# Where the two parts of a head pair's value product stand in the attention loop, and the order of four small copies

## The chip, the cores and the metric

The kernel runs on one core of a Trainium2 chip. The metric is the device time of one execution in microseconds (us). A core has TensorE (PE in the profile; PEld is its weight load), VectorE (DVE), ScalarE (ACT), GpSimd (POOL) and SyncE (SP), each with its own instruction stream, which it works through in order. TensorE writes its results to PSUM, which has eight banks.

## The reference

```
scores = q @ k.T / sqrt(64) + decay            # decay from cumsum(log f); causal mask
attn   = softmax(scores)                       # 4 batches x 8 heads, 576 x 576
x      = attn @ v                              # laid out as 2304 tokens x 512
h = x @ w_in;   x = (h * clip(h + 3, 0, 6) / 6) @ w_out
h = x @ w_in2;  out = (max(h, 0) + alpha * min(h, 0)) @ w_out2
```

All inputs are float32; both feed-forward layers have 2048 inner columns. The change touches the attention alone, in the line `x = attn @ v`.

## The kernel before

The 32 heads are worked in 16 pairs, and each pair is cut into nine **units** of query rows: four units of 128 rows for the first head, one **tail unit** that holds the last 64 rows of both heads, and four units for the second head. They are called u0 to u3, u4 (the tail) and u5 to u8 here. A unit goes through a pipeline that is spread over the steps of one loop (`for t in range(...)`). In step t each engine is given, in the order of the letters in `ORD = "TMEVDS"`:

- T, the transposes of unit t-5 on TensorE (`transposes`, line 419; the tail unit also has a small fifth one, `tq`, line 423);
- M, the negated row maximum of unit t-1 on VectorE (`maxes`, line 364);
- E, the exponential of unit t-2 on ScalarE (`exps`, line 371), which also sums each row;
- V, the copies of the transposed unit t-5 out of PSUM (`evac`): on VectorE for u3 and u8, on ScalarE for all others (`EV`);
- D, what a finished pair still needs, at fixed distances from its last unit: `recips` (RD = 3), `spread` (SD = 6; transposes `tr` and `tj` on TensorE, then three ScalarE copies, lines 456 and 460), and the value product `stage3` in two parts (PA = 7 and PB = 9);
- S, the scores of unit t on TensorE (`stage1`, lines 388 to 390, for the tail 400 to 404).

So while one pair's scores and softmax run, the pair before it is finished. In the text, "u1" to "u8" are the units of the running pair, and the value product that stands among them belongs to the pair before.

The value product's first part covers query rows 0 to 255 (four matmuls in the program), the second rows 256 to 575 (ten). Each matmul gives one head's 64 output channels, so a weight tile has 64 columns and the two heads' matmuls fill the two halves of the array (`128*64` in the profile). Everything else in the loop uses tiles of 128 columns. Most of these float32 matmuls show twice in the profile. After each part VectorE multiplies the result with the reciprocal row sums into `r` (line 480).

The eight PSUM banks are dealt out so:

- four hold scores. `score_banks` hands them out in turn, one per unit and two for the tail, ten per pair, and a score matmul waits for the exponential that last read its bank (`reader`). By that count u7 and u8 get the two banks that u4 had, u6 the bank of u3, and u5 the bank of u2;
- three form the ring `ps_pt` (tag `tp`): each unit's transposes take the next one, so do `tq`, `tr` and `tj`; a new tile waits until the tile three places earlier has been read;
- one, `ps_pv`, holds the value product.

Weight conversion and the building of the feed-forward's operands are set between these steps by tables of step numbers; in all pairs but the last ScalarE's share of them is given out behind u6's exponential. The feed-forward runs after the attention.

Of the kernel before, what the change touches and what calls it, by code (L numbers as in the profile page):

```python
# [8 lines left out]
F32 = mybir.dt.float32  # L9
# [12 lines left out]
def decay_attention_ffn2_kernel(ctx, tc, qk, v, f, wi1, wo1, wi2, wo2, alpha, out):  # L22
    nc = tc.nc
    NHEAD = qk.shape[0]
    S = f.shape[1]
# [3 lines left out]
    NP = B * NPAIR  # L29
# [11 lines left out]
    TAIL = S - 512  # L41
    PR = S - 128
    LM, LE, LT, LV = 1, 2, 5, 5
    RD, SD, PA, PB = 3, 6, 7, 9
# [16 lines left out]
    EV = (0, 0, 0, 1, 0, 0)  # L61
# [205 lines left out]
    def x_places(c, t0, t1):  # L267

        got = []
        while t0 < t1:  # L270
            p = t0 // (2 * NB)
            e, o = min(t1, (p + 1) * 2 * NB), 2 * NB * p
            view = R[p].rearrange("p (c t) -> p c t", c=KD)[:, c, t0 - o:e - o]
            got.append((view, t0, e))
            t0 = e
        return got


    def attention():
        with ExitStack() as ax:  # L280
# [28 lines left out]
            ps_pt = ax.enter_context(tc.tile_pool(name="ps_pt", bufs=3, space=PSUM))  # L309
            ps_pv = ax.enter_context(tc.tile_pool(name="ps_pv", bufs=1, space=PSUM))  # L310
# [8 lines left out]
            def load_v(p):  # L319
                vs[p] = vp.tile([128, KT, 128], F32, tag="v", name="vt")  # L320
                nc.sync.dma_start(out=vs[p], in_=v[p // NPAIR, p % NPAIR])
# [21 lines left out]
            def copy_k(h):  # L343
                q1, q2, k1, k2 = slots[h]
                if h >= 4:
                    nc.sync.dma_start(out=k2[0:64].bitcast(F32), in_=k1[0:64].bitcast(F32))
# [60 lines left out]
            def pt_tile(h):  # L407
                if h not in pts:
                    pts[h] = ptp.tile([128, (KT - 1) * PR + S], F32, tag="pt", name="pt")
                return pts[h]  # L410

            def rows(t, n, c0, cw):
                return t[:, c0:c0 + n * PR].rearrange("p (j s) -> p j s", s=PR)[:, :, 0:cw]
# [12 lines left out]
            def evac(u, tp, tq):  # L426
                p, ab, i = u
                if ab < 2:
                    copy = nc.vector.tensor_copy if EV[i] else nc.scalar.copy
                    copy(out=rows(pt_tile(2 * p + ab), i + 1, 128 * i, 128), in_=tp[:, 0:i + 1, :])  # L430
                    return
                for a in range(2):
                    copy = nc.vector.tensor_copy if EV[4 + a] else nc.scalar.copy
                    dst = pt_tile(2 * p + a)
                    copy(out=rows(dst, 4, 512, TAIL), in_=tp[:, :, 64 * a:64 * a + 64])  # L435
                    copy(out=dst[0:TAIL, 4 * PR + 512:4 * PR + S], in_=tq[0:TAIL, 0, 64 * a:64 * a + 64])

            def recips(p):

                ss = sm.pop(p)  # L440
                rc = st.tile([128, 9], F32, tag="rc", name="rc")
                nc.vector.tensor_scalar(out=rc, in0=ss, scalar1=1e-9, scalar2=None, op0=ALU.add)
                nc.vector.reciprocal(out=rc, in_=rc)
                rw = rcp.tile([128, 4, 2, 64], F32, tag="rw", name="rw")
                scaled("P", rw, rc[:, 0:8].rearrange("p (a i) -> p i a", a=2).unsqueeze(3)
                       .broadcast_to([128, 4, 2, 64]))
                rcs[p] = rw, rc

            def spread(p):

                rw, rc = rcs.pop(p)
                t = rcp.tile([128, S], F32, tag="rcb", name="rcb")
                tr = ps_pt.tile([128, 4, 128], F32, tag="tp", name="tr")
                for i in range(4):
                    nc.tensor.transpose(tr[:, i, :], rw[:, i].rearrange("p a b -> p (a b)"), ident)  # L455
                nc.scalar.copy(out=t[:, 0:512], in_=tr.rearrange("p a b -> p (a b)"))
                tj = ps_pt.tile([128, 4, 128], F32, tag="tp", name="tj")
                nc.tensor.transpose(tj[:, 0, :], rc[:, 8:9].broadcast_to([128, 128]), ident)
                for a in range(2):
                    nc.scalar.copy(out=t[64 * a:64 * a + 64, 512:S], in_=tj[64 * a:64 * a + 64, 0, 64 * a:64 * a + 64])  # L460
                rcb[p] = t

            def stage3(p, part):
                b, hp = divmod(p, NPAIR)
                vt = vs[p]
                q0, q1 = ((0, 256), (256, S))[part]
                pv = ps_pv.tile([128, 512], F32, tag="pv", name="pv")
                js = [j for j in range(KT) if 128 * j < q1]
                for j in js:
                    lo = max(q0, 128 * j)  # L470
                    kk = min(128, S - 128 * j)
                    for a in range(2):
                        nc.tensor.matmul(  # L473
                            out=pv[64 * a:64 * a + 64, lo - q0:q1 - q0],
                            lhsT=vt[0:kk, j, 64 * a:64 * a + 64],
                            rhs=pts[2 * p + a][0:kk, j * PR + lo:j * PR + q1],
                            start=(j == js[0]), stop=(j == js[-1]))
                for view, t0, t1 in x_places(hp, b * S + q0, b * S + q1):
                    c0, c1 = t0 - b * S, t1 - b * S
                    nc.vector.tensor_mul(out=view, in0=pv[:, c0 - q0:c1 - q0], in1=rcb[p][:, c0:c1])  # L480
                if part == 1:
                    for d, key in ((vs, p), (rcb, p), (pts, 2 * p), (pts, 2 * p + 1)):
                        d.pop(key)
# [48 lines left out]
            for a in range(2):  # L532
                nc.sync.dma_start(out=aq_d[a, :, 0:2, 576 - 64 * a:640 - 64 * a],
                                  in_=zero[32 * a:32 * a + 32, 0:128].rearrange("p (r c) -> p r c", r=2))
# [59 lines left out]
            for t in range(len(units) + max(LV, PB) + 1):  # L594
                now = todo.pop(t, [])
                for ch in ORD:
                    if ch == "D":
                        for fn in now:
                            fn()
                    if ch == "S" and t < len(units):  # L600
                        live[t] = stage1(units[t])
                    for c, lag, fn in (("M", LM, maxes), ("E", LE, exps)):
                        if ch == c and 0 <= t - lag < len(units):
                            live[t - lag] = fn(*live[t - lag])
                    for c, lag, fn in (("T", LT, transposes), ("V", LV, evac)):
                        if ch == c and 0 <= t - lag < len(units):
                            live[t - lag] = fn(units[t - lag], *live[t - lag])
                if t < len(units):
                    p, ab, i = units[t]
                    pos = t % 9  # L610
                    if ab == 1 and i == 3:
                        for d, fn in ((RD, lambda p=p: recips(p)), (SD, lambda p=p: spread(p)),
                                      (PA, lambda p=p: stage3(p, 0)), (PB, lambda p=p: stage3(p, 1))):
                            todo.setdefault(t + d, []).append(fn)
                    if pos == (2 if p else 8):
                        load_v(p)
                    if pos == QA and 2 * p + 2 < 2 * NP:
                        prep_head(2 * p + 2)
                        todo.setdefault(t + QL, []).append(lambda h=2 * p + 2: low_k(h))
                        todo.setdefault(t + QL, []).append(lambda h=2 * p + 2: copy_k(h))  # L620
                        todo.setdefault(t + QL + 1, []).insert(0, lambda h=2 * p + 2: low_q(h))
                        if p:
                            load_head(2 * p + 3)
                    if pos == QB and 2 * p + 3 < 2 * NP:
                        prep_head(2 * p + 3)
                        for fn, d in ((low_k, QL), (copy_k, QL), (low_q, QL if p else QL + 2)):
                            todo.setdefault(t + d, []).append(lambda fn=fn, h=2 * p + 3: fn(h))
                        if 2 * p + 4 < 2 * NP:
                            load_head(2 * p + 4)
                elif t == len(units) + LE:  # L630
                    rx.close()
                    ffn_open()
                for fn in side.pop(t, []):
                    fn()
                if t < 9:
                    idle(2)
                for _ in range(DRAIN.get(t, 0)):
                    step()
# [244 lines left out]
    def step():  # L883
        return next(runner, None)
# [57 lines left out]
```

## Time and profile before

| | |
|---|---|
| median of 3 runs | 965.91 us (965.73 to 966.28) |
| the profiled execution | 965.22 us, its span 963.4 us |
| busy, PE | 953.9 us, 99% of the span |
| busy, DVE, ACT, POOL | 698.6, 536.3 and 595.3 us |
| granted TensorE clock | 1.00 of full speed in every slice |

"Busy" of TensorE runs from the start of a matmul to a modelled end. Neighbouring matmuls overlap, so an engine that is shown as busy can still be waiting; the distance between the starts of two instructions tells more than the busy time.

### The profile page before, as it was taken

The page shows a single profiled execution, that of the slowest core. Times are in us where ns is not written, and L with a number is a line of the kernel's source. Part 1 is how long each engine was busy: PE and PEld are TensorE (multiplying, and loading weights), DVE is VectorE, ACT ScalarE, POOL GpSimd, SP SyncE. Part 2 cuts the span into 40 slices and gives each one's busy share as a digit, 9 for nine tenths or more (in the row PEclk, how much of TensorE's full clock was granted, in tenths as well). Part 3 has the DMA queues.
Part 4 walks back from the last instruction along what each step waited for, and adds up shares of the span by engine and source line. Part 5 has one row for each costly group of instructions (what it writes and reads, how often), then busy time and mean ns, then how long its engine had stood idle before and what let it go on. Part 6 is the DMA issues. An engine that isn't in the chain of part 4 may idle for free.

```text
span 963.4 us, 15758 instructions
## 1 busy us (share of the span) xinstructions
PE 953.9 (99%) x5525; PEld 858.4 (89%) x5525; DVE 698.6 (73%) x1211; ACT 536.3 (56%) x1316; POOL 595.3 (62%) x583
## 2 busy tenths in 40 slices
PE   8999999999999999999999999999999999999998
PEld 5777777789999999999999999989899898989897
DVE  7888999858687877786788565367788778535454
ACT  5788887765655555464645365545444545443231
POOL 8677989766665566585766299546555669423131
PEclk9999999999999999999999999999999999999999
DMA  6766777300443344211587723414434410344541
GB/s 206 230 188 187 217 241 228 110 30 13 173 186 133 141 186 168 84 44 34 194 318 272 277 77 120 164 46 173 186 101 173 166 64 30 111 188 159 202 164 66
DMA packets 36195, 145.79 MB, mean 151 GB/s; under 512 B 4860, under 2 KB 4860, under 8 KB 33012
## 3 DMA queue, kind: packets, MB, share of 16 engines
q1 hardware_dynamic: 36112, 144.79, 42.6%
q8 instruction: 43, 0.70, 0.3%
q14 instruction: 36, 0.29, 0.1%
q10 hardware_dynamic: 4, 0.00, 0.0%
HBM read 97.21 MB, written 43.42 MB: 146 GB/s over the span
## 4 chain that ended last, share of the span: by engine, by line
PE 93%; POOL 2%; DVE 2%; DMA 1%; issue 1%; ACT 1%; SPq 0%; POOLq 0%; DVEq 0%; ACTq 0%
PE o L772 21%; PE hA L732 20%; PE o L770 19%; PE hC L732 10%; PE hB L732 5%; PE pv L473 5%; PE tp L419 5%; PE sc L388 3%; PE sc L389 2%; PE sc L390 1%; PE sc L400 1%; PE sc L402 1%; PE tr L455 1%; POOL xl L249 1%; DVE r L241 0%
## 5 line engine op out<-in xcount | busy, mean ns | idle before, releaser
L715 POOL TENSOR_TENSOR g<-t,g 128x384 fp32r<-128x384 f32 x192 | 205.9, 1073 | 283.7 <-ACT g L714 267.3
L770 PE MATMUL o<-g,wo 128*128 128x384 f32 x1152 | 230.7, 338 | 1.2 <-POOL g L715 1.1
L732 PE MATMUL hA<-xh,wi 128*128 128x384 f32 x768 | 224.3, 337 | 0.3 <-DVE hD L746 0.3
L772 PE MATMUL o<-wo,g 128*128 128x512 f32 x864 | 223.2, 394 | 0.0
L770 PEld LDWEIGHTS o<-g,wo 128*128 128x128 f32 x1152 | 204.1, 188 | 2.2 <-POOL g L715 1.8
L714 ACT CAST g<-t 128x384 fp32r<-128x384 f32 x192 | 98.9, 515 | 176.7 <-DVE t L709 92.2
L772 PEld LDWEIGHTS o<-wo,g 128*128 128x128 f32 x864 | 160.6, 188 | 25.7
L790 DVE TENSOR_TENSOR r<-o,r 128x512 f32<-128x512 f32 x126 | 86.7, 688 | 86.2 <-PE o L772 85.7
L732 PEld LDWEIGHTS hA<-xh,wi 128*128 128x128 f32 x768 | 141.5, 188 | 3.9 <-DVE hD L746 0.6
L732 PE MATMUL hA<-xl,wi 128*128 128x384 f32 x384 | 129.5, 337 | 0.0
L779 DVE SCALAR_TENSOR_TENSOR r<-o,r 128x384 f32<-128x384 f32 x168 | 92.3, 553 | 47.0 <-PE o L770 46.2
L732 PE MATMUL hC<-xh,wi 128*128 128x384 f32 x384 | 114.1, 338 | 0.0
L371 ACT ACTIVATE p<-sc,nm 128x128 f32<-128x128 f32 (+2 forms) x144 | 80.3, 560 | 16.0 <-DVE nm L364 12.1
L364 DVE TENSOR_REDUCE nm<-sc 128x1 f32<-128x128 f32 (+2 forms) x144 | 71.1, 507 | 11.7 <-PE sc L390 7.5
L732 PEld LDWEIGHTS hA<-xl,wi 128*128 128x128 f32 x384 | 72.1, 188 | 3.2
L732 PEld LDWEIGHTS hC<-xh,wi 128*128 128x128 f32 x384 | 70.9, 188 | 2.1 <-issue 0.2
L249 POOL TENSOR_TENSOR xl<-r,xh 128x384 fp32r<-128x384 f32 x59 | 69.1, 1183 | 2.2 <-ACT xh L244 1.6
L419 PE MATMUL tp<-ident,p 128*128 128x128 f32 x384 | 67.4, 278 | 0.6 <-ACT pt L435 0.6
L737 ACT COPY s<-hA 128x384 f32<-128x384 f32 x96 | 45.9, 478 | 36.2 <-PE hA L732 35.9
L732 PE MATMUL hC<-xl,wi 128*128 128x384 f32 x192 | 64.7, 337 | 0.0
L732 PE MATMUL hB<-xh,wi 128*128 128x384 f32 x192 | 57.1, 338 | 0.0
L746 DVE TENSOR_TENSOR hC<-hC,s 128x384 f32<-128x384 f32 x48 | 27.1, 564 | 40.7 <-PE hC L732 38.8
(143 smaller groups left out, 1744.8 us busy)
## 6 DMA issues: line engine op xcount, KB each, us to landing
wid<-wi SPq DMA_DIRECT2D x24, 896.0 KB
wi<-wid SPq DMA_DIRECT2D x12, 1792.0 KB
rqk<-in_qk SPq DMA_DIRECT2D x32, 608.0 KB
raw<-in_wi SPq DMA_DIRECT2D x32, 512.0 KB
raw<-in_wo SPq DMA_DIRECT2D x32, 512.0 KB
wod<-wo SPq DMA_DIRECT2D x24, 512.0 KB
wo<-wod SPq DMA_DIRECT2D x12, 1024.0 KB
vt<-in_v SPq DMA_DIRECT2D x16, 320.0 KB
```

The lines of the kernel that those rows point to most:

```text
L249: e.tensor_sub(out=XS[k][1][:, b, c], in0=x, in1=XS[k][0][:, b, c].bitcast(F32))
L364: last = waits("V", nc.vector.tensor_reduce(out=nm, in_=src, axis=AX.X if n == 1 else AX.XY, op=ALU.max, negate=True), last)
L371: last = waits("A", nc.scalar.activation(out=o, in_=src, func=AF.Exp, bias=nm, scale=1.0, accum_out=dst), last)
L419: nc.tensor.transpose(tp[:, j, :], pt[:, 128 * j:128 * j + 128], ident)
L473: nc.tensor.matmul(out=pv[64 * a:64 * a + 64, lo - q0:q1 - q0], lhsT=vt[0:kk, j, 64 * a:64 * a + 64], rhs=pts[2 * p + a][0:kk, j * PR + lo ...
L714: nc.scalar.copy(out=gt[n][i][:, 0], in_=hold["g"])
L715: nc.gpsimd.tensor_sub(out=gt[n][i][:, 1], in0=hold["g"], in1=gt[n][i][:, 0].bitcast(F32))
L732: nc.tensor.matmul(out=h, lhsT=a, rhs=b[:, x, kc], start=new and kc + e == 0, stop=kc == KH - 1 and e == 2, skip_group_check=not new)
L770: nc.tensor.matmul(out=o[:, 0:NB], lhsT=a[:, cs], rhs=b, start=st, stop=sp)
L772: nc.tensor.matmul(out=o, lhsT=b[:, cs], rhs=a, start=st, stop=sp)
L779: later(0, lambda: nc.vector.scalar_tensor_tensor(out=acc, in0=o[:, 0:NB], scalar=1.0 / 6.0, in1=acc, op0=ALU.mult, op1=ALU.add))
L790: nc.vector.tensor_add(out=acc, in0=o, in1=acc)
```

## The change

The first part of the value product moves from step PA = 7 to step PB = 9, directly ahead of the second, for all pairs but the last. Its result no longer goes to the bank of `ps_pv` but to the next bank of the ring `ps_pt` (name `pw`); the last pair keeps both parts as they were. Independently, `evac` copies the tail unit out in another order: first both halves of `tp`, then both halves of `tq`, where it was `tp`, `tq`, `tp`, `tq`.

```diff
                 for a in range(2):
                     copy = nc.vector.tensor_copy if EV[4 + a] else nc.scalar.copy
-                    dst = pt_tile(2 * p + a)
-                    copy(out=rows(dst, 4, 512, TAIL), in_=tp[:, :, 64 * a:64 * a + 64])
-                    copy(out=dst[0:TAIL, 4 * PR + 512:4 * PR + S], in_=tq[0:TAIL, 0, 64 * a:64 * a + 64])
+                    copy(out=rows(pt_tile(2 * p + a), 4, 512, TAIL), in_=tp[:, :, 64 * a:64 * a + 64])
+                for a in range(2):
+                    copy = nc.vector.tensor_copy if EV[4 + a] else nc.scalar.copy
+                    copy(out=pt_tile(2 * p + a)[0:TAIL, 4 * PR + 512:4 * PR + S], in_=tq[0:TAIL, 0, 64 * a:64 * a + 64])
...
-                pv = ps_pv.tile([128, 512], F32, tag="pv", name="pv")
+                if part == 1 or p == NP - 1:
+                    pv = ps_pv.tile([128, 512], F32, tag="pv", name="pv")
+                else:
+                    pv = ps_pt.tile([128, 4, 128], F32, tag="tp", name="pw").rearrange("p a b -> p (a b)")
...
                         for d, fn in ((RD, lambda p=p: recips(p)), (SD, lambda p=p: spread(p)),
-                                      (PA, lambda p=p: stage3(p, 0)), (PB, lambda p=p: stage3(p, 1))):
+                                      (PB if p < NP - 1 else PA, lambda p=p: stage3(p, 0)), (PB, lambda p=p: stage3(p, 1))):
```

On TensorE, before, from u1's transposes to u7's scores (the first of the 15 places; `sc` are scores, `128x384` in a score's row marks u7, and the waits name engines' semaphores):

```order
L419 MATMUL tp<-ident,p 128x128 [waits Activation_49]
L419 MATMUL tp<-ident,p 128x128
L473 MATMUL pv<-pt,vt 64x256 [waits DMAHW0_49]
L473 MATMUL pv<-pt,vt 64x256
L473 MATMUL pv<-pt,vt 64x128 x2
L388 MATMUL sc<-k_363,q_361 128x256
L389 MATMUL sc<-k_364,q_362 128x256
L390 LDWEIGHTS identb
L390 MATMUL sc<-maskb,identb 128x128
L419 MATMUL tp<-ident,p 128x128 [waits Activation_49]
L419 MATMUL tp<-ident,p 128x128 x2
L388 MATMUL sc<-k_363,q_361 128x384 [waits Activation_49]
```

The same stretch of TensorE's stream in the changed kernel:

```order
L419 MATMUL tp<-ident,p 128x128 [waits Activation_49]
L419 MATMUL tp<-ident,p 128x128
L388 MATMUL sc<-k_363,q_361 128x256
L389 MATMUL sc<-k_364,q_362 128x256
L390 LDWEIGHTS identb
L390 MATMUL sc<-maskb,identb 128x128
L419 MATMUL tp<-ident,p 128x128 [waits Activation_49]
L419 MATMUL tp<-ident,p 128x128 x2
L388 MATMUL sc<-k_363,q_361 128x384 [waits Activation_49]
```

The four value matmuls between u1's transposes and u6's scores are gone; all that stood behind them moves up, and u7's scores keep their wait for ScalarE.

Further down TensorE's stream, the end of u3's transposes and what follows, in the changed kernel:

```order
L419 MATMUL tp<-ident,p 128x128 x3
L477 MATMUL pw<-pt,vt 64x256 [waits DMAHW0_49,Activation_49]
L477 MATMUL pw<-pt,vt 64x256
L477 MATMUL pw<-pt,vt 64x128 x2
L477 MATMUL pv<-pt,vt 64x320 x6
L477 MATMUL pv<-pt,vt 64x192 x2
L477 MATMUL pv<-pt,vt 64x64 x2
L388 MATMUL sc<-k_363,q_361 128x512
```

Before, the second part stood there alone, and its first matmul waited for VectorE, which had to read the first part out of the same bank.

On ScalarE, around the tail unit's copies, before:

```order
L371 ACTIVATE p,sm<-sc,nm 128x384 [waits DVE_49,PE_49,Activation_49]
L435 COPY pt<-tp 128x4x64 [waits PE_49]
L436 COPY pt<-tq 64x64 [waits PE_49]
L435 COPY pt<-tp 128x4x64 [waits DMAHW3_49,DMAHW2_49,DMAHW6_49,DMAHW1_49,DMAHW7_49,DMAHW0_49,Pool_49]
L436 COPY pt<-tq 64x64
L371 ACTIVATE p,sm<-sc,nm 128x512 [waits DVE_49,Activation_49]
```

And there in the changed kernel:

```order
L371 ACTIVATE p,sm<-sc,nm 128x384 [waits DVE_49,PE_49,Activation_49]
L434 COPY pt<-tp 128x4x64 [waits PE_49]
L434 COPY pt<-tp 128x4x64 [waits DMAHW3_49,DMAHW2_49,DMAHW6_49,DMAHW1_49,DMAHW7_49,DMAHW0_49,Pool_49]
L437 COPY pt<-tq 64x64 [waits PE_49]
L437 COPY pt<-tq 64x64
L371 ACTIVATE p,sm<-sc,nm 128x512 [waits DVE_49,Activation_49]
```

The last reader of the tail's `tp` bank is now the second copy instead of the third; the four copies and what follows them are the same.

## Rows read from the trace of the kernel before

**Rows 1.** The profile's page: busy time, share of the span and instructions of each engine.

```profile
PE 953.9 (99%) x5525; PEld 858.4 (89%) x5525; DVE 698.6 (73%) x1211; ACT 536.3 (56%) x1316; POOL 595.3 (62%) x583
```

**Rows 2.** Window of one pair: length, each engine's busy time (instructions), clock, DMA.

```profile
77.66:89.13 11.47, 11.47 (x95) 8.42 (x92) 10.04 (x21) 9.60 (x33) 8.90 (x10) 1.00 0.69 214
```

**Rows 3.** Timeline of TensorE, one pair: start, length, line, names, count [idle before].

```profile
66.98 0.23 PE L390 MATMUL sc<-maskb,identb 128*128 128x128 bf16 x1
67.19 0.44 PE L419 MATMUL tp<-ident,p 128*128 128x128 f32 x2
67.38 0.42 PE L388 MATMUL sc<-k,q 128*128 128x384 f32 x1
...
70.51 0.60 PE L455 MATMUL tr<-ident,rw 128*128 128x128 f32 x4
...
71.37 0.39 PE L419 MATMUL tp<-ident,p 128*128 128x128 f32 x2
71.69 0.87 PE L473 MATMUL pv<-pt,vt 128*64 128x256 f32 x8
72.49 0.38 PE L388 MATMUL sc<-k,q 128*128 128x256 f32 x1
...
72.83 0.23 PE L390 MATMUL sc<-maskb,identb 128*128 128x128 bf16 x1
72.90 0.50 PE L419 MATMUL tp<-ident,p 128*128 128x128 f32 x3
73.15 0.42 PE L388 MATMUL sc<-k,q 128*128 128x384 f32 x1
...
73.66 0.61 PE L419 MATMUL tp<-ident,p 128*128 128x128 f32 x4
74.20 2.42 PE L473 MATMUL pv<-pt,vt 128*64 128x320 f32 x20
76.55 0.50 PE L388 MATMUL sc<-k,q 128*128 128x512 f32 x1
```

**Rows 4.** The same timeline in narrow windows, which show starts inside both value products.

```profile
71.96 0.39 PE L473 MATMUL pv<-pt,vt 128*64 128x256 f32 x2
...
72.17 0.39 PE L473 MATMUL pv<-pt,vt 128*64 128x128 f32 x4
...
72.28 0.28 PE L473 MATMUL pv<-pt,vt 128*64 128x128 f32 x2
...
74.52 0.44 PE L473 MATMUL pv<-pt,vt 128*64 128x320 f32 x2
...
74.79 0.44 PE L473 MATMUL pv<-pt,vt 128*64 128x320 f32 x2
```

**Rows 5.** Timeline of TensorE's weight loads where the first part begins.

```profile
71.69 0.63 PEld L473 LDWEIGHTS pv<-pt,vt 128*64 128x64 f32 x8 [0.17 <-issue]
```

**Rows 6.** Timeline of ScalarE in the same pair.

```profile
66.39 0.37 ACT L435 COPY pt<-tp 128x256 f32<-128x256 f32 x1 [1.88 <-PE tp L419]
66.66 0.21 ACT L436 COPY pt<-tq 64x64 f32<-64x64 f32 x1
66.77 0.37 ACT L435 COPY pt<-tp 128x256 f32<-128x256 f32 x1
...
71.15 0.59 ACT L456 COPY rcb<-tr 128x512 f32<-128x512 f32 x1 [0.17 <-PE tr L455]
71.63 0.42 ACT L460 COPY rcb<-tj 64x64 f32<-64x64 f32 x2
72.08 0.74 ACT L371 ACTIVATE p<-sc,nm 128x576 f32<-128x576 f32 x1
72.72 0.20 ACT L371 ACTIVATION_READ_ACCUMULATOR p<-sc,nm 128x1 f32 x1
72.81 0.36 ACT L430 COPY pt<-tp 128x256 f32<-128x256 f32 x1
```

**Rows 7.** Timeline of VectorE in the same pair.

```profile
75.64 0.67 DVE L430 COPY pt<-tp 128x512 f32<-128x512 f32 x1
```

## The prediction

> **What bounds the kernel now.** I read the page first: TensorE is shown as busy for 99% of the span [rows 1], so a gain or a loss has to come from TensorE's own sequence. The window of one pair shows 11.47 us, TensorE busy in all of it, VectorE for 10.04, ScalarE for 9.60 and POOL for 8.90 [rows 2]. In this stretch busy proves little, since matmuls overlap in the profile. I therefore went on to TensorE's timeline of one pair and read distances between starts [rows 3], to ScalarE's timeline of the same pair [rows 6], and asked of each wait who releases it and how much earlier than needed.
>
> Two things are to be seen there. First, TensorE flows almost without waits, with one exception: u6's transposes start 0.21 after the mask matmul ahead of them (66.98 to 67.19), where 0.07 is usual (72.83 to 72.90) [rows 3]. They wait for ScalarE: the third of the tail's four copies ends at 66.77 + 0.37 = 67.14, and they start 0.05 later [rows 3, 6]. Second, u7's scores, at 73.15, come only just after what they need. Their bank is the one that u4's exponential reads. That exponential starts at 72.08, and its accumulator read ends at 72.72 + 0.20 = 72.92 [rows 6]. With the same 0.05 from release to start, u7's scores could begin at 72.97 at the earliest: 0.18 of spare time, no more.
>
> **The change part by part.**
>
> *Taking part one out of its old place.* Without it, u6's scores follow u1's two transposes directly. Three transposes take 0.25 up to the next scores (72.90 to 73.15), a pair of them that had to wait takes 0.19 (67.19 to 67.38) [rows 3]; I take 0.15 for a pair that flows. So u6's scores move from 72.49 to 71.37 + 0.15 = 71.52, and u7's, which follow 0.66 behind (72.49 to 73.15), would be ready to start at 72.18: 0.97 earlier [rows 3].
>
> *But they must wait.* ScalarE's way to u4's exponential isn't moved at all. It starts with `tr` at 70.51, which stands ahead of the change on TensorE [rows 3]. ScalarE is idle 0.17 until `tr` is there, and then works without a break: the copy of `tr` (71.15), two of `tj` (71.63), the exponential (72.08), its accumulator read (72.72) [rows 6]. The order there is the same afterwards. So u7's scores start at 72.97 instead of 72.18 and TensorE stands for 0.79. Of the 0.97 taken out, 0.18 is gained. Behind the waiting matmul stand u3's transposes, the whole value product and u8's scores; nothing else of TensorE can go ahead.
>
> *Putting part one ahead of part two.* The first part's steps start at 71.69, 71.96, 72.17 and 72.28 [rows 3, 4]: 0.27, 0.21, 0.11, and 0.11 once more for the second of two equal steps, together 0.70. Part two's first step loses the start-up that a stream's first has, 0.32 against 0.27 (74.20, 74.52, 74.79) [rows 3, 4]: 0.05 back. So everything from u8's scores on comes 0.65 later than the start of u7's scores would have it. I let the last steps of part two stand as they are.
>
> The Trainium skill (TensorEngine Tiling (Array Packing), Key Properties) says that a change of tiling mode drains TensorE. The trace agrees: 0.17 of idle weight load ahead of the first 64-column tile [rows 5]. By that rule alone the merged parts save one change into 64-column tiles and one back, and the change pays; it is the first rival below.
>
> *The waits that are new.* `pw` takes the ring bank of u1's transposes, whose copy ends at 72.81 + 0.36 = 73.17 [rows 6]; `pw` cannot start before 72.97 + 1.05 = 74.02 (73.15 to 74.20 is 1.05 [rows 3]), so this is covered by 0.8. `tq` now waits for VectorE's copy of u3, which ends at 75.64 + 0.67 = 76.31 [rows 7], before u8's scores start at 76.55 [rows 3]; `tq` stands behind these and comes later than now, so this is covered too. u5's transposes wait for VectorE's multiply of `pw`, which stands right behind that copy; if this cover were gone, each 0.1 would cost 15 x 0.1 = 1.5 us. VectorE's multiplies are the same work in other places.
>
> *The tail's copies.* The second copy of `tp` takes the slot that starts at 66.66, ends 0.37 later at 67.03 instead of 67.14, and lets u6's transposes go 0.11 earlier. The four copies together take as long as before. ScalarE was idle for 1.88 until the tail's transposes came [rows 6], so its start is TensorE's doing and the 0.11 is real there. Bounds: 0 in pairs where ScalarE runs late from there to u4's exponential, and 0.14 + 0.04 if the whole stall went (0.21 against 0.07, and the pair of transposes at 0.19 against the 0.15 taken above).
>
> **The sum.** Per changed pair -0.18 + 0.65 = +0.47; 15 pairs: +7.05. The tail's copies: 16 x -0.11 = -1.76. Together **+5.3 us**. The profiled execution took 965.22 us, 1.8 more than its span, so it would be 970.5; the median of the three runs is 0.7 above it, and from there I predict **971.2**. I assume that the delay reaches the end undiminished: the loop's step numbers order all side work, and the feed-forward's TensorE work follows as one block.
>
> Bounds of the unknown prices: were u7's scores released by the exponential itself (72.08 + 0.74 = 72.82) rather than by its accumulator read, 0.28 would be gained instead of 0.18, and with 0.18 for the tail the sum is 15 x 0.37 - 16 x 0.18 = +2.7. Were nothing gained by the tail, and u7's scores 0.05 slower after a wait as u6's transposes are, it is 15 x 0.52 = +7.8. The case itself so runs from 968.6 to 973.7; I take the middle, as both rows that it rests on show start-to-release times directly.
>
> **The rivals.**
>
> *The merged stream pays (faster).* If u7's scores didn't have to wait, each pair would gain 0.97 - 0.65 = 0.32, and 15 x 0.32 + 1.76 = 6.6 us come off: 959.3. It is decided at one place: u4's exponential would have to be read by 72.13, that is 0.79 earlier against `tr` than now. For it speaks that the bank's wait costs nothing today. Against it: the copies of `tr` and `tj` and the exponential stand back to back on ScalarE [rows 6], and the count of banks leaves u7 no other. Chance 0.13. This is where the skill's drain rule would lead.
>
> *The two effects meet (no change).* The longer pair gives VectorE and POOL time, and if small stalls elsewhere shrink by some 0.35 a pair, the balance is near zero: 964 to 968. Against it: outside u6's transposes the timeline shows no such stall to shrink [rows 3]. Chance 0.07.
>
> *Worse than forecast (slower).* If `pw` to `pv` costs a drain as well, because the bank changes, the stream's saving is lost: part one would cost 0.97 in its new place instead of 0.65, 15 x 0.32 = 4.8 more, 976.0. Against it: both parts use the same 64-column tiles, and the eight weight loads of part one show no idle time among them, only ahead of the first [rows 5]. Chance 0.06.
>
> Forecast: 0.74. A measurement tells about 0.2%, 1.9 us, from no change. The forecast and the last rival are slower by more than that: 0.80; same 0.07; faster 0.13. The range takes the forecast's own 968.6 to 973.7 and goes out to 967.2 and 974.2, into the neighbours' near sides, for 8 in 10.
>
> **What the profile will show.** If I am right: the waits list "PE sc L388" waiting for "ACT p L371" 15 times, some 0.5 us each as shown (the modelled end of the transposes ahead hides 0.2 to 0.3 of the 0.79); pair windows of about 11.8 us; u6's transposes some 0.1 after the mask matmul; `pw` steps of 0.27, 0.21, 0.11, 0.11 and no 0.32 for the first step of `pv`. Wrong if u7's scores start directly behind u2's transposes (the first rival), if u5's transposes wait for VectorE's multiply of `pw`, or if the pairs get longer and the end doesn't move.

## The result and the profile after

The changed kernel is slower: 972.85 us, the median of 6 runs (972.55 to 973.73), against 965.83 us in the 6 runs of the kernel before that stood beside them (965.53 to 966.31). The ratio is 1.0075, its interval 1.0065 to 1.0086. The profiled execution has a span of 970.8 us, 7.4 more than before.

The page's busy line of the changed kernel answers to [rows 1]. No engine has more instructions than before, and TensorE is busy for 0.3 us less, but the program is 7 us longer. VectorE alone is busy for clearly longer, by 3.8 us, a first sign of what follows below.

```profile
PE 953.6 (98%) x5525; PEld 859.3 (89%) x5525; DVE 702.4 (72%) x1211; ACT 534.3 (55%) x1316; POOL 594.0 (61%) x583
```

The small transpose `tq` occurs once in each pair, at the same place, so the distance from one `tq` to the next on TensorE is the length of a pair. (Its tile too has 64 columns, `128*64` in its row, not 128 as was said of everything but the value product; it is the same in both kernels.) The view of that tile gives the number of its instructions, their shortest, median and longest duration in ns, and the first and the last start in us. After the change:

```profile
L423 PE MATMUL tq<-ident,p x16: 272/273/273, 19.8 to 200.2; 128*64 128x128 f32 x16
```

The first start is at 19.7 before and 19.8 after, the last at 193.0 and 200.2. So the 15 pairs between took 173.3 us and now take 180.4: 7.1 of the 7.4 us are made there, and the feed-forward carries them to the end undiminished.

TensorE's timeline of the changed kernel, the same pair as in [rows 3]:

```profile
67.45 0.27 PE L423 MATMUL tq<-ident,p 128*64 128x128 f32 x1
...
68.23 0.23 PE L390 MATMUL sc<-maskb,identb 128*128 128x128 bf16 x1
68.35 0.44 PE L419 MATMUL tp<-ident,p 128*128 128x128 f32 x2
...
73.03 0.50 PE L419 MATMUL tp<-ident,p 128*128 128x128 f32 x3
74.08 0.45 PE L388 MATMUL sc<-k,q 128*128 128x384 f32 x1 [0.56 <-ACT p L371]
...
74.61 0.61 PE L419 MATMUL tp<-ident,p 128*128 128x128 f32 x4
75.15 0.87 PE L477 MATMUL pw<-pt,vt 128*64 128x256 f32 x8
75.85 2.37 PE L477 MATMUL pv<-pt,vt 128*64 128x320 f32 x20
78.15 0.50 PE L388 MATMUL sc<-k,q 128*128 128x512 f32 x1
...
79.25 0.27 PE L423 MATMUL tq<-ident,p 128*64 128x128 f32 x1
```

u7's scores (128x384) start at 74.08. Three transposes that flow take 0.25 [rows 3], so they could have started at 73.28: TensorE stands for 0.80. The bracket says for whom, ScalarE's line 371, and shows 0.56, because the modelled end of the transposes covers the rest. ScalarE's timeline of the same stretch, which answers to [rows 6]:

```profile
72.26 0.59 ACT L457 COPY rcb<-tr 128x512 f32<-128x512 f32 x1
72.75 0.42 ACT L461 COPY rcb<-tj 64x64 f32<-64x64 f32 x2
73.20 0.74 ACT L371 ACTIVATE p<-sc,nm 128x576 f32<-128x576 f32 x1
73.83 0.20 ACT L371 ACTIVATION_READ_ACCUMULATOR p<-sc,nm 128x1 f32 x1
```

The copies of `tr` and `tj`, u4's exponential and its accumulator read stand without a break, and the read ends at 73.83 + 0.20 = 74.03, 0.05 before u7's scores start. The view of waits, pairs 2 to 16 (engine and line, for whom it waited: us in total, times, longest), has it 15 times; before, no scores of line 388 waited for ScalarE there:

```profile
PEld sc L388 <- ACT p L371: 11.8, 15, 0.8
...
PE sc L388 <- ACT p L371: 8.2, 15, 0.6
```

This pair takes 79.25 - 67.45 = 11.80 us instead of 11.47 [rows 2]. That is +0.33, and fifteen times 0.33 is only 5.0 of the 7.1. The first pair apart (12.31, before 12.11), those up to the seventh are all like this one (11.79 to 11.84); of the eight later ones five are longer still, up to 12.76. Where the rest comes from is seen on VectorE in one of these. VectorE's timeline of the changed kernel; line 357 computes the low part of a coming head's queries, line 352 on POOL that of its keys:

```profile
150.05 0.68 DVE L430 COPY pt<-tp 128x512 f32<-128x512 f32 x1
150.65 0.41 DVE L484 TENSOR_TENSOR r<-pw,rcb 128x256 f32<-128x256 f32 x1
150.98 0.54 DVE L484 TENSOR_TENSOR r<-pv,rcb 128x128 f32<-128x128 f32 x2
151.44 0.68 DVE L364 TENSOR_REDUCE nm<-sc 128x1 f32<-128x512 f32 x1
152.03 1.99 DVE L357 SCALAR_TENSOR_TENSOR q<-rqk,q 64x640 fp32r<-64x640 f32 x1
153.95 0.60 DVE L364 TENSOR_REDUCE nm<-sc 128x1 f32<-128x128 f32 x2
```

POOL at that time, in the changed kernel:

```profile
151.93 1.42 POOL L352 TENSOR_TENSOR k<-rqk,k 64x576 fp32r<-64x576 f32 x1
```

The same place in the kernel before, VectorE and then POOL:

```profile
145.89 0.68 DVE L430 COPY pt<-tp 128x512 f32<-128x512 f32 x1
146.48 0.54 DVE L480 TENSOR_TENSOR r<-pv,rcb 128x128 f32<-128x128 f32 x2
146.94 0.68 DVE L364 TENSOR_REDUCE nm<-sc 128x1 f32<-128x512 f32 x1
147.54 0.83 DVE L357 SCALAR_TENSOR_TENSOR q<-rqk,q 64x640 fp32r<-64x640 f32 x1
```

```profile
147.77 1.89 POOL L352 TENSOR_TENSOR k<-rqk,k 64x576 fp32r<-64x576 f32 x1
```

Before, VectorE began first (147.54 against 147.77), took 0.83, and POOL's subtraction was drawn out to 1.89. After, the multiply of `pw` stands in the way (0.33 from its start to the next), VectorE begins second (152.03 against 151.93), takes 1.99 itself, and POOL needs only 1.42. POOL has time to spare and VectorE here has none: behind line 357 stands u0's maximum, and for it wait u0's exponential on ScalarE and then, because it holds their bank, the tail's scores on TensorE. ScalarE and TensorE in the changed kernel:

```profile
154.32 0.37 ACT L371 ACTIVATE p<-sc,nm 128x128 f32<-128x128 f32 x1 [1.09 <-DVE nm L364]
```

```profile
153.87 0.61 PE L419 MATMUL tp<-ident,p 128*128 128x128 f32 x4
154.83 0.40 PE L400 MATMUL sc<-k,q 128*128 128x288 f32 x1 [0.36 <-ACT p L371]
```

Four transposes that flow take 0.36 up to the tail's scores (69.92 to 70.28 in the pair shown first), so they should have begun at 154.23 and are 0.60 late. This pair is 0.96 longer than 11.80; the other 0.36 comes in small steps up to 157.50, at the tail's further scores and the transposes behind them.

The order turns in the same way in all of these places. The table gives, for the seven pairs that begin with the eighth to the fourteenth `tq`, the distance from the start of VectorE's copy of u3 (line 430) to POOL's line 352 and to VectorE's line 357, the duration of this line 357, and the length of the pair, all in us, read from the timelines of the three engines:

| before: to L352 | to L357 | L357 takes | pair | after: to L352 | to L357 | L357 takes | pair |
|---|---|---|---|---|---|---|---|
| 1.60 | 1.59 | 0.80 | 11.47 | 1.61 | 1.99 | 1.71 | 12.18 |
| 2.14 | 2.05 | 0.81 | 11.47 | 2.16 | 2.64 | 1.61 | 12.09 |
| 2.43 | 2.02 | 1.01 | 11.47 | 2.42 | 2.62 | 1.89 | 12.35 |
| 2.16 | 2.19 | 2.06 | 12.04 | 2.15 | 2.88 | 1.36 | 11.86 |
| 1.89 | 1.66 | 0.83 | 11.47 | 1.89 | 1.99 | 1.99 | 12.76 |
| 2.15 | 2.02 | 0.81 | 11.47 | 2.15 | 2.88 | 1.35 | 11.84 |
| 2.16 | 1.86 | 0.90 | 11.47 | 2.15 | 2.35 | 1.89 | 12.35 |

POOL's distance from the copy is the same to 0.02; VectorE's has grown by 0.33 to 0.86, because the multiply of `pw` and 0.65 us more of TensorE's stream now lie between the copy of u3 and u8's maximum. Before, VectorE came second in one of the seven, which is also the one long pair; after, in all. The longer its line 357, the longer the pair.

### The profile page after: what moved, and what is told of

It is laid out like the page before. It is cut to its first block, busy times and chain, and to the rows that moved or that the text cites. A ratio compares the mean times of both kernels' runs of the same rounds, so it can differ in the third digit from the quotient of the medians.

```text
span 970.8 us, 15796 instructions
## 1 busy us (share of the span) xinstructions
PE 953.6 (98%) x5525; PEld 859.3 (89%) x5525; DVE 702.4 (72%) x1211; ACT 534.3 (55%) x1316; POOL 594.0 (61%) x583
## 4 chain that ended last, share of the span: by engine, by line
PE 88%; ACT 4%; DVE 3%; issue 2%; POOL 1%; DMA 1%; DVEq 0%; ACTq 0%; POOLq 0%
PE o L776 21%; PE hA L736 20%; PE o L774 19%; PE hC L736 10%; PE hB L736 5%; PE pv L477 3%; PE tp L419 3%; ACT p L371 2%; PE sc L388 2%; PE sc L389 1%; PE pw L477 1%; ACT rcb L461 1%; PE sc L390 1%; PE sc L400 1%; POOL xl L249 1%
## 5 line engine op out<-in xcount | busy, mean ns | idle before, releaser
L388 PE MATMUL sc<-k,q 128*128 128x256 f32 (+2 forms) x128 | 53.6, 419 | 8.8 <-ACT p L371 8.2
```

The source lines that it names most:

```text
L388: waits("T", nc.tensor.matmul(out=sc[:, 0:n], lhsT=q1[:, qs], rhs=k1[:, 0:n], start=True, stop=False), *free)
```

## Experiments

**The theory** at the start was that of the prediction: u7's scores wait for u4's exponential, so most of what is taken out of the old place is lost there, and the merged stream lies behind. **Its rivals**: that the merged stream itself saves less than thought (a price between the two banks), and that the loss comes from VectorE and POOL. Each kernel is compared with runs of the kernel before that stood beside it, and an edit is shown against the changed kernel where nothing else is said; "pair" is the distance between two `tq`, and an undisturbed pair is one without a long line 357.

**The tail's copies alone** (the kernel before with the new order of the four copies):

```diff
-                if part == 1 or p == NP - 1:
-                    pv = ps_pv.tile([128, 512], F32, tag="pv", name="pv")
-                else:
-                    pv = ps_pt.tile([128, 4, 128], F32, tag="tp", name="pw").rearrange("p a b -> p (a b)")
+                pv = ps_pv.tile([128, 512], F32, tag="pv", name="pv")
...
-                                      (PB if p < NP - 1 else PA, lambda p=p: stage3(p, 0)), (PB, lambda p=p: stage3(p, 1))):
+                                      (PA, lambda p=p: stage3(p, 0)), (PB, lambda p=p: stage3(p, 1))):
```

> The kernel before with the new copy order alone; the value product stays as it was. My theory: u6's transposes start 0.11 instead of 0.21 us after the mask matmul, nothing else moves, 16 x -0.11 = -1.7 us, some 964.1. The rival, that ScalarE's chain as a whole sets the pace and the slot is only shifted: no change.

Measured: 964.17 us against 965.34, ratio 0.9988 [0.9979, 0.9996]. TensorE's timeline of this kernel at u6's transposes:

```profile
66.84 0.23 PE L390 MATMUL sc<-maskb,identb 128*128 128x128 bf16 x1
66.95 0.44 PE L419 MATMUL tp<-ident,p 128*128 128x128 f32 x2
```

u6's transposes stand 0.11 behind the mask matmul instead of 0.21 [rows 3], and an undisturbed pair takes 11.33 us, 0.14 less than 11.47. Five of the later pairs take 11.57 to 11.85, which keeps the whole gain at 1.2 us and not at 16 x 0.14 = 2.2.

**The merging alone** (the changed kernel with the old order of the copies):

```diff
-                    copy(out=rows(pt_tile(2 * p + a), 4, 512, TAIL), in_=tp[:, :, 64 * a:64 * a + 64])
-                for a in range(2):
-                    copy = nc.vector.tensor_copy if EV[4 + a] else nc.scalar.copy
-                    copy(out=pt_tile(2 * p + a)[0:TAIL, 4 * PR + 512:4 * PR + S], in_=tq[0:TAIL, 0, 64 * a:64 * a + 64])
+                    dst = pt_tile(2 * p + a)
+                    copy(out=rows(dst, 4, 512, TAIL), in_=tp[:, :, 64 * a:64 * a + 64])
+                    copy(out=dst[0:TAIL, 4 * PR + 512:4 * PR + S], in_=tq[0:TAIL, 0, 64 * a:64 * a + 64])
```

> The changed kernel with the old copy order: the merged value product alone. My theory: u7's scores wait for u4's exponential in 15 pairs as in the changed kernel, and the 1.7 us of the copies are missing: some 974.5. The rival, that the new copy order is what holds ScalarE up: faster than the changed kernel, 970 or less.

Measured: 974.29 against 965.34, ratio 1.009 [1.0076, 1.0103]. The wait of u7's scores is there with the same sums (8.2 us in 15 waits), and an undisturbed pair takes 11.94, that is 11.47 + 0.47. So in undisturbed pairs the two parts of the change add up, +0.47 and -0.14 a pair. In the profiled execution the first `tq` came at 21.6, 1.8 later than in the changed kernel and before any changed pair; this belongs to the 974.29. The stretch from 12 to 14 us shows where it comes from (the view of that window, this kernel first, then the changed one; the third number from the end is TensorE's granted clock):

```profile
12.00:14.00 2.00, 2.00 (x7) 1.03 (x6) 0.56 (x1) 1.17 (x4) 0.58 (x2) 0.50 0.85 292
12.00:14.00 2.00, 2.00 (x14) 1.43 (x12) 1.25 (x2) 1.14 (x5) 0.56 (x2) 1.00 0.94 331
```

The clock stood at 0.50 of full speed, the lower of its two levels (1.2 GHz), and TensorE has 7 matmuls there instead of 14. Before that TensorE had stood idle for 1.52 and 1.15 us, waiting for operands of the first heads; in the kernel before, where the clock stayed at 1.00, for 1.50 and 0.86. Why it fell here and not there isn't shown. It differs between executions of one kernel: the one of the five with a mean clock of 1.000 took 973.49 us, the others, with 0.997 or 0.998, 974.06 to 974.33.

**Both parts at the old step 7** (which takes u7's wait away, since the long stream then lies ahead of u6's scores):

```diff
-                                      (PB if p < NP - 1 else PA, lambda p=p: stage3(p, 0)), (PB, lambda p=p: stage3(p, 1))):
+                                      (PA, lambda p=p: stage3(p, 0)), (PA if p < NP - 1 else PB, lambda p=p: stage3(p, 1))):
```

> The changed kernel with both parts at step 7, behind u1's transposes, instead of step 9: the same merged stream and ring bank, but u7's scores come 1.6 us later than in the kernel before, long after u4's exponential is read. My theory: no wait of u7's scores, and the merged stream pays 15 x 0.32 plus 1.7 for the copies: 6.5 us faster than before, some 959.3. The rival, that a merged stream or its ring bank costs time by itself wherever it stands: 966 or more.

Measured: 978.34, ratio 1.013 [1.0116, 1.0144]: a miss, and the slowest but one. u7's wait is gone, and the second and third pair take 11.18 and 11.27, less than 11.33. From then on they take 12 and more. Three lines of the view of waits of this kernel name what came instead:

```profile
ACT pt L430 <- PE tp L419: 30.8, 14, 2.2
DVE r L484 <- PE pv L477: 22.3, 14, 1.8
...
PE tp L419 <- DVE pt L430: 11.4, 12, 1.4
```

VectorE comes to the second part's multiply early and stands before it, up to 1.8 us a time, with its maxima, its conversions and the copy of u3 queued behind. Then u5's transposes wait for that copy: the timeline of TensorE has them at

```profile
80.18 0.33 PE L419 MATMUL tp<-ident,p 128*128 128x128 f32 x1 [1.00 <-DVE pt L430]
```

**Both parts at step 8**, a step later than the last kernel:

```diff
-                                      (PB if p < NP - 1 else PA, lambda p=p: stage3(p, 0)), (PB, lambda p=p: stage3(p, 1))):
+                                      (PA + 1 if p < NP - 1 else PA, lambda p=p: stage3(p, 0)), (PA + 1 if p < NP - 1 else PB, lambda p=p: stage3(p, 1))):
```

> Both parts at step 8, between u2's transposes and u7's scores. My theory: u7's scores stand directly behind the value product, so u4's exponential has 3 us more; no wait, some 959.3 as with step 7. The rival, as there: 966 or more. A third view, that VectorE's order around the multiplies decides: the two differ by 2 us or more.

Measured: 979.91, ratio 1.0153 [1.0134, 1.0173]. Neither the forecast of 959.3 nor the third view, 2 us or more between steps 7 and 8, is borne out: the two medians are 1.6 apart. The first two pairs take 11.01, the shortest of the study, the later ones 11.5 to 14.5. In the profiled execution the clock stood at 0.50 from 12 to 14 us here too, and the first `tq` came at 21.3; its 981.49 us hold that. The waits of this kernel are the same two as in the last one and, larger still, ScalarE's for VectorE's maxima:

```profile
ACT p L371 <- DVE nm L364: 36.8, 12, 3.7
DVE r L484 <- PE pv L477: 21.7, 13, 1.8
...
PE tp L419 <- DVE pt L430: 13.3, 12, 1.5
```

**Both parts at step 7, VectorE's multiplies one step later**, so that VectorE doesn't stand before them, and the conversion work (letters f, s, j and g of its tables) mostly one step earlier; the two were not tried apart:

```diff
...
+                if p == NP - 1:
+                    mul()
+                else:
+                    held.setdefault(p, []).append(mul)
...
-                                      (PB if p < NP - 1 else PA, lambda p=p: stage3(p, 0)), (PB, lambda p=p: stage3(p, 1))):
+                                      (PA, lambda p=p: stage3(p, 0)), (PA if p < NP - 1 else PB, lambda p=p: stage3(p, 1)),
+                                      (PA + 1, lambda p=p: muls(p))):
```

> Both parts at step 7 as in the run that was slow, but the multiplies one step later on VectorE, and VectorE's conversion work of the next step drawn ahead of them, so that VectorE has work while TensorE is in the value product. My theory now: at step 7 the wait of u7's scores is gone, and what cost 12 us there was VectorE standing 1.7 us per pair behind a multiply that waited for part two; with that gone the stream pays: 959 to 962. The rival, that VectorE is full and the pair cannot be shorter than before: 966 or more.

Measured: 970.58, ratio 1.0055 [1.0043, 1.0068]; 7.8 us less than with the multiplies in step 7, but not the 959 to 962 of the theory. The second, third and fifth pair take 11.23 to 11.29, the others 11.6 to 12.6, and TensorE now waits for the next engine, ScalarE, whose copies of the tail unit come late (waits of this kernel):

```profile
ACT pt L430 <- PE tp L419: 33.1, 15, 2.2
...
PE tp L419 <- ACT pt L434: 4.7, 10, 0.9
```

These 4.7 us are little more than half of what the pairs take beyond 11.29 each (177.6 us for the 15); the rest was not followed.

**A copy of `tj` done twice**, once in the changed kernel and once in the kernel before, each shown against itself without it. This lengthens ScalarE's way to u4's exponential by one small copy and nothing else; both got the same line:

```diff
+                nc.scalar.copy(out=t[64:128, 512:S], in_=tj[64:128, 0, 64:128])
                 rcb[p] = t
```

> The changed kernel with one of the two small copies of tj done twice, so that u4's exponential comes 0.21 us later on ScalarE. My theory, that u7's scores wait for ScalarE's chain from tr to u4's exponential: 15 x 0.21 = 3.2 us slower than the changed kernel, some 976. The rival, that VectorE's order or the stream itself costs the time: within 0.5 of the changed kernel.

> The kernel before with the same copy done twice. My theory: 0.21 us against 0.18 to 0.2 of spare time, so 0 to 0.5 us slower, at most 966.4. The rival, that any work on ScalarE there costs time in both kernels: 3.2 us slower, some 969.

Measured: the changed kernel with the extra copy took 975.56 against 965.39 (1.0104 [1.009, 1.0118]), so its loss grew from 7.0 to 10.2 us; the kernel before with it took 966.6 (1.0011 [1.0002, 1.002]), 1.2 more than without. That is above the 0 to 0.5 expected and far below the rival's 3.2. The pairs say it more plainly. ScalarE in the kernel before with the copy (line 461 is the extra one):

```profile
72.53 0.21 ACT L461 COPY rcb<-tj 64x64 f32<-64x64 f32 x1
72.76 0.74 ACT L371 ACTIVATE p<-sc,nm 128x576 f32<-128x576 f32 x1
73.40 0.19 ACT L371 ACTIVATION_READ_ACCUMULATOR p<-sc,nm 128x1 f32 x1
```

The copy's slot is 0.23. In the changed kernel an undisturbed pair went from 11.80 to 12.04, by the whole 0.24. In the kernel before it went from 11.47 to 11.53, by 0.06: the 0.18 of spare time ahead of u7's scores took the rest. (Fifteen times 0.06 is 0.9; the first pair and two of the later ones are longer besides.) So both numbers on which the prediction's main term stood, no spare time after and 0.18 before, are shown by adding to them.

**The two `tj` copies behind u4's exponential** (changed kernel, otherwise as it is), which gives ScalarE's way back the time of both:

```diff
-                for a in range(2):
-                    nc.scalar.copy(out=t[64 * a:64 * a + 64, 512:S], in_=tj[64 * a:64 * a + 64, 0, 64 * a:64 * a + 64])
...
+                def tails():
+                    for a in range(2):
+                        nc.scalar.copy(out=t[64 * a:64 * a + 64, 512:S], in_=tj[64 * a:64 * a + 64, 0, 64 * a:64 * a + 64])
+                return tails
...
-                        for d, fn in ((RD, lambda p=p: recips(p)), (SD, lambda p=p: spread(p)),
+                        for d, fn in ((RD, lambda p=p: recips(p)), (SD, lambda p=p, t=t: todo.setdefault(t + SD + 1, []).insert(0, spread(p))),
```

> The changed kernel with the two copies of tj behind u4's exponential instead of ahead of it, so that the exponential comes 0.43 us earlier. My theory: the wait of u7's scores shrinks from 0.56 as shown by 0.43, 15 x 0.43 = 6.4 us come off: some 966.5. The rival, that the wait is fixed by VectorE: within 1 us of 972.9.

Measured: 968.0 against 965.39, ratio 1.0029 [1.0019, 1.0039]; the loss fell from 7.0 to 2.6 us. ScalarE and then TensorE in this kernel:

```profile
71.17 0.59 ACT L457 COPY rcb<-tr 128x512 f32<-128x512 f32 x1
71.65 0.75 ACT L371 ACTIVATE p<-sc,nm 128x576 f32<-128x576 f32 x1
72.28 0.20 ACT L371 ACTIVATION_READ_ACCUMULATOR p<-sc,nm 128x1 f32 x1
```

```profile
71.93 0.50 PE L419 MATMUL tp<-ident,p 128*128 128x128 f32 x3
72.54 0.45 PE L388 MATMUL sc<-k,q 128*128 128x384 f32 x1
```

The exponential follows directly on the copy of `tr`, and u7's scores start 0.61 behind u2's transposes, where it was 1.05 (73.03 to 74.08). An undisturbed pair takes 11.36, 0.44 less than 11.80. That is still not below 11.33, since 0.36 of the wait is left. Fifteen times 0.44 would be 6.6 and not 4.4: in six later pairs the first line 357 takes 1.69 to 2.03, and these take 11.74 to 12.76, while all others but the first take 11.35 to 11.40.

**The low part of the queries one step earlier** (changed kernel; line 357 of every pair's later head moves to the head of the step before, out of POOL's way):

```diff
...
-                        for fn, d in ((low_k, QL), (copy_k, QL), (low_q, QL if p else QL + 2)):
+                        for fn, d in ((low_k, QL), (copy_k, QL)):
...
+                        todo.setdefault(t + (QL - 1 if p else QL + 2), []).insert(0 if p else 99, lambda h=2 * p + 3: low_q(h))
```

> The changed kernel with VectorE's subtraction for the second head's query (line 357) one step earlier, ahead of the multiplies, so that it no longer falls into the same step as POOL's subtraction for the key (line 352). My theory: in the pairs from the eighth on, where it takes 1.4 to 2.0 us instead of 0.81, it holds up u0's maximum and by it the tail's scores; the pairs of 12.1 to 12.8 us come back to 11.8, some 2.8 us come off: 970.1. The rival, that the collision only moves to another place: 972 or more.

Measured: 970.65 against 965.75, ratio 1.005 [1.0038, 1.0063], so a loss of 4.9 us instead of 7.0. The wait of u7's scores is unchanged in sum (8.2 us, 15 times). Line 357 in the changed kernel, in the view of groups (busy time and mean ns), and then in this one:

```profile
L357 DVE SCALAR_TENSOR_TENSOR q<-rqk,q 64x640 fp32r<-64x640 f32 x32 | 40.1, 1252 | 0.3 <-ACT q L90 0.2
```

```profile
L357 DVE SCALAR_TENSOR_TENSOR q<-rqk,q 64x640 fp32r<-64x640 f32 x32 | 34.5, 1079 | 0.1
```

The pairs are now 11.78 to 11.90 except the first and one of 12.16. The view of `tq` gives 19.9 to 198.1:

```profile
L423 PE MATMUL tq<-ident,p x16: 272/273/273, 19.9 to 198.1; 128*64 128x128 f32 x16
```

So 178.2 us for the 15 pairs instead of 180.4. These 2.2 us are the part of the loss that the wait of u7's scores and the merged stream didn't explain.

**The same move added to three other kernels**: to the one with the late `tj` copies, to the one with both parts at step 7 and late multiplies, and to the one with the copies' order alone. The edit is the one above each time.

> The kernel with tj's copies behind u4's exponential (968.0), and the subtraction of line 357 one step earlier. There the undisturbed pairs take 11.36 us and six disturbed ones 11.74 to 12.76. My theory: all pairs near 11.36, 4.4 us come off: some 963.6. The rival: 967 or more.

> Both parts at step 7 with the late multiplies (970.6), and the subtraction one step earlier. Its first pairs take 11.25 us, its later ones 11.6 to 12.6. If line 357 alone spoils the later pairs: some 962. The rival, that VectorE and ScalarE are too full there for TensorE to run through 3 us of value product in one piece: 968 or more.

> The kernel before with the new copy order (964.2), and the subtraction one step earlier. Five of its pairs take 11.57 to 11.85 instead of 11.33. My theory: 1 to 1.5 us come off, 962.7 to 963.2. The rival, that the subtraction then delays the multiply of part one: 964 or more.

Measured: 968.48 (1.0027 [1.0017, 1.0037]), 977.67 (1.0115 [1.0099, 1.013]) and 965.46 (0.9998 [0.9989, 1.0006]). None is faster for it, all three came out as their rivals said, and the second lost 6.7 us more than without the move; some 2 us of these go with the clock, which stood at 0.50 from 12 to 14 us in its profiled execution (979.45 us, against 975.39 in the one execution with a mean clock of 1.000). In the first the moved line 357 takes 1.46 to 1.72 in three places, and eight pairs of 11.58 to 12.6 remain; in the second the pairs grow to 14.5 and u7's scores wait for ScalarE again. So the move helped in the changed kernel and in none of the others. What the later pairs of these kernels wait for was not settled.

Of all versions only the copies' order alone lies below the kernel before with its whole interval, by 0.12%, which is less than the 0.2% that a measurement tells here with any safety.

## Why the prediction came out as it did

The predicted 971.2 us was 1.65 below the measured 972.85; as a difference, +5.3 was predicted and +7.0 came. Taken by its own steps:

- **u7's scores must wait.** Right in place and size: 0.80 of standing against 0.79, released by the accumulator read with 0.05 from its end, 15 times 0.5 or so as the view shows it. The extra copy and the late copies showed it as a cause: the pair moved by +0.24 and -0.44 with ScalarE's way to that exponential, and in the kernel before only by what exceeded 0.18.
- **The merged stream.** `pw` to `pv` takes 0.70 (75.15 to 75.85), as summed from the four steps, and from the first `pv` to u8's scores 2.30 instead of 2.35 [rows 3], the 0.05 that was taken off. So the merging costs +0.47 in an undisturbed pair, 11.80 against 11.33, the figure of the sum. The rival with a second drain between the banks is refuted. The Trainium skill (TensorEngine Tiling (Array Packing), Key Properties) speaks of a drain at a change of tiling mode; no run here shows the drain by itself, only that some early pairs with the whole stream at step 7 or 8 take 11.01 to 11.29, less than 11.33.
- **The tail's copies.** Right in kind, small in size: 0.14 in an undisturbed pair instead of 0.11, 16 x 0.14 = 2.2 instead of 1.76. The stall itself fell by the 0.10 that the rows show (0.21 to 0.11); where the other 0.04 lies was not followed. Over the whole program the copies alone gave 1.2, since five later pairs lost part of it.
- **"VectorE's multiplies are the same work in other places."** This is the step that failed: the sum put it at nothing. Its one named risk, that u5's transposes wait for the multiply of `pw`, didn't show. But the multiplies' place mattered: with the multiply of `pw` and the longer stream ahead of it, line 357 comes 0.33 to 0.86 later, behind POOL's line 352, and it takes 1.35 to 1.99 instead of 0.80 to 1.01 in six of seven later pairs. How much of that the multiply makes and how much the longer stream was not tried apart. Moving it away took 2.2 us off the 15 pairs (180.4 to 178.2). The sum without it, 15 x 0.47 - 16 x 0.14 = 4.8, is what that kernel shows, 970.65 - 965.75 = 4.9. With the 2.2 the sum is 7.0, the loss that was measured. That 972.85 still lies in the stated range is in part luck: the range went up for a tail without gain and a slower start after the wait, and neither came; what filled it was this term.
- **The first rival** (the merged stream pays if u7 needn't wait). Its condition was tried with the stream at steps 7 and 8. The saving is there in a few early pairs alone: 11.01 to 11.29. (The pairs of 11.01 follow the low clock at the start, which may have given the other engines a lead.) It wasn't kept in any of these kernels: VectorE, which works in order, stands before the product of the long stream, and TensorE then waits for what is queued behind; with the multiplies moved back it waits for ScalarE's copies. These waits were missing from that rival's price of 959.3.
- **The second rival** (the two effects meet) had the sign of the side effect wrong: the longer pair gave VectorE and POOL no relief, but a worse order.

What stays open: what ties POOL's line 352 so closely to VectorE's copy of u3, why the clock fell at the start in the profiled executions of three kernels (the merging alone, both parts at step 8, both at step 7 with line 357 moved), which made their first tail unit some 1.5 to 1.8 us later, and what lengthens the later pairs where line 357 no longer does.

## What to carry to other kernels

Before work is taken out ahead of a waiting instruction, ask how much earlier its operand could be there: here 0.18 us of spare time, not the 0.97 taken out, set the gain, while the cost in the new place was paid in full. Work that "only moves" on an engine that isn't the bound moves what stands behind it against the other engines too; look for two instructions on VectorE and POOL that overlap in time and slow each other, and ask which will start first afterwards. A long block on the bounding engine saved its own start-up here, but it starved engines that work in order, because one of them stood before the block's result with other work queued behind. And when two versions differ by a us or two, look at the granted clock of each stretch before looking for a cause in the code.

## What the runs showed of the hardware

VectorE's line 357 and POOL's line 352 exclude each other almost wholly, and the one that starts second pays. Second by 0.10, 0.20, 0.38 and 0.48 us, line 357 took 1.99, 1.89, 1.71 and 1.61: in each of these it ends 2.09 after POOL's start, as if it did its own 0.81 only from 1.28 after that start on, and POOL, first, takes its usual 1.42. With VectorE first, POOL took 1.88 to 2.07 in the kernel before and VectorE 0.80 to 1.01 in six of the seven pairs of the table. The 1.01 has the same cause: that line 357 started at 123.83, while POOL's line 241, which stands ahead of line 352, ran until 124.16. The Trainium skill (SBUF — State Buffer, Who interferes with whom) says that a VectorE instruction with two SBUF inputs contends with a POOL instruction that reads SBUF, and that the order of issue decides who is blocked. The trace agrees, with these numbers. The summed time of the two lines changes little, 36.0 and 48.9 us before, 40.1 and 46.1 after: a tenth of a microsecond decides mainly who pays.

A second thing: an exponential that also sums its rows let its bank go only with the accumulator read behind it. In the trace it is that read which signals to TensorE, and u7's scores started 0.05 after its end (74.03 to 74.08), in the changed kernel, and likewise with the extra copy in it (75.33 to 75.38); with the late `tj` copies it was 0.06 (72.48 to 72.54).
